# A Mamba-2 scan with a PReLU MLP: steps of the first group put in another order

## Chip, cores and metric

The kernel runs on one core of one Trainium2 chip. The metric is the device time of one execution, in microseconds (us); the time of a kernel is the median over several runs. The core has engines with a queue each: TensorE (PE, with its weight loads shown as PEld), VectorE (DVE), ScalarE (ACT), GpSimd (POOL), and SyncE (SP), which here only issues DMAs. Engines tell each other through semaphores that a step is done.

## What is computed

Two stages, the second on the output of the first. Cut to what matters:

```python
# x (4, 8, 768, 32), a (4, 8, 768), B and C (4, 8, 768, 16); chunks of 32 in the reference
for each chunk:
    cum = cumsum(log(clip(a, 1e-6, 1)))
    M = (C @ B^T) * exp(cum_i - cum_j) * (i >= j)       # per batch and head
    y = M @ x + (C @ state) * exp(cum)
    state = exp(sum(log a)) * state + sum_j B_j x_j exp(cum_end - cum_j)
# y, (batch, seq, heads * 32) = 3072 tokens x 256, goes into
h = y @ w_in                                            # 256 x 2048
g = max(h, 0) + alpha * min(h, 0)                       # PReLU with a slope for each column
out = g @ w_out                                         # 2048 x 256
```

## The kernel before

Everything is float32. The kernel works in chunks of 128 tokens. Two chunks are a **pair** (`pair(gp)`, gp = 0 to 11; six chunks, three pairs, to a batch), and two pairs, 512 tokens, are a **group** of the MLP (0 to 5). Pairs 0 and 1 feed group 0, pairs 2 and 3 feed group 1. Each engine runs its instructions in the order in which the code writes them (`manual_schedule`), so a line that is moved in the code is moved in the queues of all engines that it uses. The tile pools set only which buffer an allocation gets, and with it whose readers it waits for.

`pair(gp)` is a generator; `ssm(gp, n)` runs it up to its n-th next `yield`. For pairs 2 and 3 its steps are these:

1. *Transposes* of B and C on PE (L469), a copy of the result to `bc` on ACT (L472), the two masked copies `cz` on ACT (L484); then `pair_loads` makes `bn`, B times the decay to the chunk's end, on POOL (L385).
2. *Scans*: `decays(0)` and `decays(1)`, each four scans on DVE (L438), write the decay matrices `dec` of one chunk each, from `abc`, which a DMA has spread over the partitions.
3. *States*: `added` multiplies `xt` and `bn` on PE (L519), `states` brings the state forward on ACT (L544) and DVE (L547) and masks it on POOL (`sm`, L550), `c_decayed` makes `cd` on POOL (L487).
4. *Gram*: `products_bc`, eight matmuls of C and B into four tiles (L564); the fourth tile, for r = 3, is one of the two `hp` buffers.
5. *Products*: four multiplications of `dec` with the Gram tiles on DVE (L600), with a `yield` after the second; the order is r = 3, 2, 1, 0.
6. *y*: matmuls into two tiles (L616 for the state's part, L623 for `dec`), and copies to `xT`, the MLP's input, on ACT (L630).

The weights arrive in 16 **pieces** of 512 KB, in float64, and are turned into float32 on the chip. Pieces 0, 1 and 2 are `w_in` columns, and from there `w_out` and `w_in` take turns: the fourth piece is the first of `w_out`, the seventh is the fifth of `w_in`. A piece of `w_in` or `w_out` holds two of the 16 blocks f of d_ff. Its conversion has two parts. `convert_a` is the first: an absolute value (`wt`, L218) and a scaled copy of the lower bits (`wg`, L225 or L228) on ACT, and a clamp of `wt` on POOL (L220). `convert` is the rest: two steps on DVE (`wr`, L238 and L239) and an addition on POOL (L261), which writes the weights. `convert_next` takes the next piece, runs `convert` on it, then, unless `first=False`, `convert_a` on the piece two further on, and then lets SP load the piece six further on into the `raw` buffer that has come free (L202).

The first group is multiplied block by block. `hidden_two` does two blocks f for 256 tokens (L657): its matmuls, ACT's scaling by alpha (L663), and, in the function that it returns, the rest of the PReLU on DVE (L669). `hidden(0, f)` does one block for 512 tokens: two wide matmuls into an `hp` buffer, of which there are two (L642), ACT's scaling (L645) and DVE's maximum (L646). `output(f)` multiplies a block with `w_out` (L680). The loop over f from 4 to 15 writes, in this order: the loads of a pair and of `a`'s rows, a step of pair 2 for f up to 10, a step of pair 3 from f = 9 on, `hidden(0, f)`, `convert_next()`, `output(f - 4)`, and in four places a sum of weights on POOL (`weight_sums`, L709), whose tile is taken from the `raw` buffers.

`rows_clamp`, `rows_scan` and `rows_out` (L339 to L363) turn the second half of `a`'s rows into products: five instructions on DVE (L339, L346, L348, L358, L360) and two DMAs on SP (L363). Their results are read again by the loads of pair 6 and later. From group 1 on, `quad` and `product` do the MLP with seven products in place of eight (L766, L741).

Of the kernel before, what the change touches and what calls it, by code (L numbers as in the profile page):

```python
# [22 lines left out]
def kernel(  # L23
# [33 lines left out]
    Q = 128  # L57
# [35 lines left out]
    gp = ctx.enter_context(tc.tile_pool(name="gp", bufs=16))  # L93
# [6 lines left out]
    def bank(i):  # L100


        return ps_q.tile([P, 512], F32, name="bank", tag=f"q{i}")
# [5 lines left out]
    def ss_tile():  # L109
        if early[0] is None:  # L110
            return ps_s.tile([P, 512], F32, name="ss")
        early[0] += 1
        i = early[0] % (3 if ident_p else 4)
        return ps_s.tile([P, 512], F32, name="ss") if i < 2 else bank(i)
# [211 lines left out]
    held = {}  # L326
# [9 lines left out]
    def rows_clamp(i):  # L336
        rows = loads.pop(("r", i))
        d0 = prep.tile([RW, Q + 1], F32, name="r0")
        nc.vector.tensor_scalar(out=d0[:, :Q], in0=rows, scalar1=1e-6, scalar2=1.0,  # L339
                                op0=ALU.max, op1=ALU.min)  # L340
        held[i] = d0

    def rows_scan(i):

        d0 = held[i]
        nc.vector.memset(d0[:, Q:], 0.0)  # L346
        pr = prep.tile([RW, Q], F32, name="pr")
        nc.vector.tensor_tensor_scan(out=pr[:, ::-1], data0=d0[:, 1:][:, ::-1],  # L348
                                     data1=ends[:RW, ::-1], initial=0.0,
                                     op0=ALU.mult, op1=ALU.add)  # L350
        return pr
# [60 lines left out]
    def spare():  # L412

        return ps_h.tile([P, GT], F32, name="hp", tag="hp")

    def pair(gp):
# [7 lines left out]
        def decays(k):  # L424

            if abc:
                for w in range(2):
                    half_decays(k, w)
                return
            for w, t in enumerate(ahead.pop(k, None) or spread(z, k)):  # L430
                ws = slice(512 * w, 512 * w + 512)
                nc.vector.tensor_tensor_scan(out=dv[:, k, ws], data0=t, data1=ident_h[:, ws],
                                             initial=0.0, op0=ALU.mult, op1=ALU.add)

        def half_decays(k, w):
            for i in range(2):
                hs = slice((2 * w + i) * 2 * Q, (2 * w + i + 1) * 2 * Q)
                nc.vector.tensor_tensor_scan(out=dv[:, k, hs], data0=abc[k][:, hs],  # L438
                                             data1=ident_p[0], initial=0.0, op0=ALU.mult,
                                             op1=ALU.add)  # L440
# [36 lines left out]
        def spread_c():  # L477
            for e in range(2):
                o = cz[:, e].rearrange("p k t -> p (k t)")
                if gp == 0 and e == 1:  # L480
                    nc.gpsimd.tensor_scalar(out=o, in0=ct, scalar1=par[:, e : e + 1],
                                            scalar2=None, op0=ALU.mult)
                else:
                    nc.scalar.mul(o, ct, par[:, e : e + 1])  # L484

        def c_decayed():
            nc.gpsimd.tensor_tensor(out=cd.rearrange("p k t -> p (k t)"), in0=ct, in1=pf,  # L487
                                    op=ALU.mult)

        fine = gp >= 2 * GC // 2  # L490
        if not fine:
            spread_c()
        if gp == 0:
            rows_turn(0, held.pop("pr"))
            dps = spare()
# [3 lines left out]
        if gp == 1:  # L499
            c_decayed()  # L500
            dps = spare()
# [12 lines left out]
        def added(dps):  # L514
            dps = dps.rearrange("p (k m) -> p k m", m=P)
            for k in range(nk):
                for w in range(KC):
                    ws = slice(64 * w, 64 * w + 64)
                    nc.tensor.matmul(dps[ws, k], bn[:, k, ws], xt[:, k, w * P : (w + 1) * P],  # L519
                                     start=True, stop=True, tile_position=(0, 64 * w),  # L520
                                     skip_group_check=True)
            return dps

        if fine:
            for k in range(2):
                for w in range(2):
                    half_decays(k, w)
                    if k == 1 and w == 1:
                        spread_c()
                    yield  # L530
        else:
            decays(0)
            if gp == 1:
                dps = added(dps)
            if gp:
                yield
            if gp != 1:
                decays(1)

        def states(dps):  # L540
            for k in range(nk):
                old = state.get(b)
                if old is None:
                    nc.scalar.copy(out=new[:, k], in_=dps[:, k])  # L544
                else:
                    e = (k + 1) * Q - 1
                    nc.vector.scalar_tensor_tensor(out=new[:, k], in0=old, scalar=pf[:, e : e + 1],  # L547
                                                   in1=dps[:, k], op0=ALU.mult, op1=ALU.add)
                state[b] = new[:, k]
            nc.gpsimd.tensor_tensor(out=sm[:, :nk], in0=new[:, :nk],  # L550
                                    in1=hmask.unsqueeze(1).to_broadcast([P, nk, P]), op=ALU.mult)
            st.extend(sm[:, k] for k in range(nk))
            masked[b] = st[-1]

# [18 lines left out]
        def times(out, g):  # L575
            nc.gpsimd.tensor_tensor(out=out, in0=g, in1=out, op=ALU.mult)

        if gp == 0:
            gram = products_bc()
            dps = added(dps)  # L580
            yield
            c_decayed()
            times(dec[:, :, :2], one_less(gram))
        elif gp == 1:
            decays(1)
            gram = products_bc()
            g0 = one_less(gram)
            states(dps)
            times(dec[:, :, :2], g0)
        else:  # L590
            if not fine:
                yield
            states(added(ss_tile()))
            c_decayed()
            yield
            gram = products_bc()
        for i, r in enumerate(r for r in ((2, 3, 0, 1) if fine else (3, 2, 1, 0) if gp > 1 else range(4))
# [51 lines left out]
    def hidden_two(g, f, t0, hp):  # L649


        nt = GT // 2
        ts = slice(t0, t0 + nt)
        for i in range(2):
            fs = slice((f + i) * P, (f + i + 1) * P)
            for k in range(KC):
                nc.tensor.matmul(hp[:, i * nt : (i + 1) * nt], w_in[:, k, fs],  # L657
                                 xts[g][:, k, ts], start=(i == 0 and k == 0),
                                 stop=(k == KC - 1), skip_group_check=True)
        for i in range(2):  # L660
            if t0 == 0:
                gts[g, f + i] = gp.tile([P, GT], F32, name="gt")
            nc.scalar.mul(gts[g, f + i][:, ts], hp[:, i * nt : (i + 1) * nt],  # L663
                          s_alpha[:, f + i : f + i + 1])

        def rest():
            for i in range(2):
                gt = gts[g, f + i][:, ts]
                nc.vector.scalar_tensor_tensor(  # L669
                    out=gt, in0=hp[:, i * nt : (i + 1) * nt], scalar=s_mul[:, f + i : f + i + 1],  # L670
                    in1=gt, op0=ALU.mult, op1=ALU.max)
        return rest
# [233 lines left out]
    pieces = in_pieces[:2]  # L906
# [9 lines left out]
    def convert_next(first=True, **kw):  # L916


        i = done[0]
        if i < len(pieces):  # L920
            convert(*pieces[i], **kw)
            if first and i and i + 2 < len(pieces):
                convert_a(*pieces[i + 2])
            if loaded[0] == i + 6:
                load_next()
        done[0] += 1
# [13 lines left out]
    FIRST = 4  # L940
# [11 lines left out]
    prelus = [hidden_two(0, 0, 0, spare())]  # L952
# [6 lines left out]
    prelus[1]()  # L959
    ssm(1)  # L960
    convert_a(*pieces[3])
    prelus = [hidden_two(0, 0, 2 * Q, spare())]
    prelus[0]()
    prelus = [hidden_two(0, 2, 2 * Q, spare())]
    convert_a(*pieces[4])
    convert_next(first=False)
    prelus[0]()
    identity_bank()
    convert_a(*pieces[5])
    convert_next()  # L970
    in_steps = {8: 0, 10: 1, 12: 2, 14: 3}
    for f in range(FIRST, NF):
        if f in (5, 10):
            load_pair(3 + f // 10)
        if f == 5:
            load_rows(1)
        if f == 9:
            rows_clamp(1)
            held["pr"] = rows_scan(1)
            rows_out(1)  # L980
        if f <= 10:
            ssm(2)
        if f >= 9:
            ssm(3)
        hidden(0, f)
        convert_next()
        output(f - FIRST)
        if f in in_steps:
            weight_sums(wi, in_sums, 0, in_steps[f])
# [89 lines left out]
```

## Time and profile before

| what | value |
|---|---|
| median of 6 runs | 377.41 us |
| single runs | 376.75, 376.77, 377.04, 377.79, 378.97, 379.03 us |
| profiled execution | 376.77 us |
| its span, first to last instruction | 375.0 us |
| granted TensorE clock | 0.999 |
| bytes moved by DMA | 30.71 MB, mean 82 GB/s |

The span by stretches, in us, each of 15 us:

| stretch | PE busy | DVE busy | ACT busy | POOL busy | share of the DMA engines |
|---|---|---|---|---|---|
| 15 to 30 | 14.28 | 11.86 | 8.65 | 10.12 | 0.94 |
| 30 to 45 | 13.03 | 10.68 | 11.86 | 7.94 | 0.80 |
| 45 to 60 | 14.07 | 14.24 | 9.22 | 9.14 | 0.90 |
| 60 to 75 | 15.00 | 13.69 | 8.11 | 11.59 | 0.92 |
| 75 to 90 | 15.00 | 10.85 | 5.17 | 12.28 | 0.23 |

The loop over f runs from about 30 to 84 us. A line of a timeline gives the start and the length of one instruction, or of several of one kind that follow each other (xN), its engine, line and operation, the tile written and the tiles read, their shapes, and in brackets the idle time of the engine before it and what ended that. The listed length of an instruction runs into the next one, so the time that a step takes from the engine is the difference between two starts. A matmul's end is modelled.

### The profile page before, as it was taken

The page shows a single profiled execution, that of the slowest core. Times are in us where ns is not written, and L with a number is a line of the kernel's source. Part 1 is how long each engine was busy: PE and PEld are TensorE (multiplying, and loading weights), DVE is VectorE, ACT ScalarE, POOL GpSimd, SP SyncE. Part 2 cuts the span into 40 slices and gives each one's busy share as a digit, 9 for nine tenths or more (in the row PEclk, how much of TensorE's full clock was granted, in tenths as well). Part 3 has the DMA queues.
Part 4 walks back from the last instruction along what each step waited for, and adds up shares of the span by engine and source line. Part 5 has one row for each costly group of instructions (what it writes and reads, how often), then busy time and mean ns, then how long its engine had stood idle before and what let it go on. Part 6 is the DMA issues. An engine that isn't in the chain of part 4 may idle for free.

```text
span 375.0 us, 6178 instructions
## 1 busy us (share of the span) xinstructions
PE 365.4 (97%) x2223; PEld 294.5 (79%) x2223; DVE 242.6 (65%) x461; ACT 179.6 (48%) x384; POOL 203.2 (54%) x212
## 2 busy tenths in 40 slices
PE   8898999999999999999999999999999999999996
PEld 8675556668878788788788788788788888888884
DVE  7985899877547737747737847637847744544364
ACT  2658665526354444444445545435525525553541
POOL 4965475878857835625555435456354355264512
PEclk9999999999999999999999999999999999999999
DMA  7999697811008701002802702801801001001003
GB/s 157 226 211 354 132 307 160 170 46 58 28 26 172 140 3 56 2 0 45 167 3 48 162 2 39 173 0 30 154 29 27 3 0 20 12 0 30 1 0 84
DMA packets 121878, 30.71 MB, mean 82 GB/s; under 512 B 93736, under 2 KB 117752, under 8 KB 121848
## 3 DMA queue, kind: packets, MB, share of 16 engines
q1 hardware_dynamic: 116736, 29.74, 35.6%
q10 hardware_dynamic: 5112, 0.59, 1.1%
q8 instruction: 17, 0.28, 0.3%
q14 instruction: 13, 0.11, 0.1%
HBM read 26.98 MB, written 3.34 MB: 81 GB/s over the span
## 4 chain that ended last, share of the span: by engine, by line
PE 87%; DVE 5%; DMA 2%; POOL 2%; ACT 1%; issue 1%; POOLq 0%; DVEq 0%; ACTq 0%
PE hp L766 33%; PE bank L741 32%; PE bank L680 5%; PE hp L642 3%; PE ss L623 2%; DMA raw<-in_moe_w_in_dram 2%; PE ss L564 2%; PE ss L616 1%; DVE dec L438 1%; PE ss L519 1%; PE hp L564 1%; PE hp L657 1%; PE ss L469 1%; PE hp L270 1%; DVE wr L239 1%
## 5 line engine op out<-in xcount | busy, mean ns | idle before, releaser
L809 POOL TENSOR_TENSOR gt<-gt 128x512 f32<-128x512 f32 x58 | 73.6, 1270 | 31.7 <-DVE gt L751 24.8
L751 DVE SCALAR_TENSOR_TENSOR gt<-hp,s_mul,gt 128x256 f32<-128x256 f32 x120 | 52.6, 480 | 47.7 <-ACT gt L749 46.7
L741 PE MATMUL bank<-gt,w_out 128*128 128x256 f32 x320 | 82.5, 382 | 0.4 <-ACT o_sb L687 0.4
L749 ACT ACTIVATE gt<-hp,s_alpha 128x256 f32<-128x256 f32 x120 | 50.3, 470 | 47.2 <-PE hp L766 32.9
L741 PEld LDWEIGHTS bank<-gt,w_out 128*128 128x128 f32 x320 | 60.0, 190 | 11.2 <-issue 2.3
L800 POOL TENSOR_TENSOR gt<-gt 128x512 f32<-128x512 f32 x20 | 25.4, 1270 | 78.2 <-DVE gt L751 78.2
L741 PE MATMUL bank<-gt,ws 128*128 128x256 f32 x240 | 58.3, 379 | 0.0
L741 PEld LDWEIGHTS bank<-gt,ws 128*128 128x128 f32 x240 | 45.1, 190 | 5.8
L438 DVE TENSOR_TENSOR_SCAN dec<-abc,bank 128x256 f32<-128x256 f32 x80 | 48.1, 661 | 0.0
L766 PE MATMUL hp<-xs,w_in 128*128 128x256 f32 x160 | 42.8, 390 | 0.0
L766 PE MATMUL hp<-xT,w_in 128*128 128x256 f32 x160 | 41.9, 384 | 0.0
L766 PE MATMUL hp<-xs,ws 128*128 128x256 f32 x160 | 41.1, 379 | 0.0
L785 DVE TENSOR_TENSOR hp<-hp,u 128x512 f32<-128x512 f32 x20 | 14.0, 700 | 39.6 <-ACT u L783 39.6
L774 ACT COPY m<-hp 128x512 f32<-128x512 f32 x20 | 11.7, 586 | 51.5 <-PE hp L766 51.5
L766 PEld LDWEIGHTS hp<-xs,w_in 128*128 128x128 f32 x160 | 28.7, 189 | 7.7 <-issue 3.3
L766 PEld LDWEIGHTS hp<-xs,ws 128*128 128x128 f32 x160 | 30.4, 190 | 4.1
L766 PEld LDWEIGHTS hp<-xT,w_in 128*128 128x128 f32 x160 | 29.7, 190 | 5.0 <-issue 1.4
L680 PEld LDWEIGHTS bank<-w_out,gt 128*128 128x128 f32 x128 | 24.1, 190 | 11.4 <-issue 4.9
L680 PE MATMUL bank<-w_out,gt 128*128 128x256 f32 x128 | 30.7, 381 | 2.0 <-POOL w_out L261 2.0
L789 DVE TENSOR_TENSOR c<-hp,m 128x512 f32<-128x512 f32 x20 | 13.6, 682 | 19.2 <-PE hp L766 19.2
L642 PE MATMUL hp<-xT,w_in 128*128 128x512 f32 x48 | 23.2, 605 | 0.0
L783 ACT COPY u<-hp 128x512 f32<-128x512 f32 x20 | 11.7, 585 | 23.0 <-PE hp L766 23.0
(155 smaller groups left out, 555.1 us busy)
## 6 DMA issues: line engine op xcount, KB each, us to landing
abc<-z SPq DMA_DIRECT2D x20, 512.0 KB, 5.2
raw<-in_moe_w_in_dram SPq DMA_DIRECT2D x8, 512.0 KB, 4.8
raw<-in_moe_w_out_dram SPq DMA_DIRECT2D x8, 512.0 KB, 6.2
xt<-in_x_dram SPq DMA_DIRECT2D x24, 128.0 KB, 2.7
out_dram<-o_sb SPq DMA_DIRECT2D x32, 64.0 KB, 1.9
nat<-in_B_dram SPq DMA_DIRECT2D x22, 64.0 KB, 2.7
nat<-in_C_dram SPq DMA_DIRECT2D x22, 64.0 KB, 3.6
ap<-pf SPq DMA_DIRECT2D x11, 128.0 KB
```

Of the source, the lines that this page charges most:

```text
L438: nc.vector.tensor_tensor_scan(out=dv[:, k, hs], data0=abc[k][:, hs], data1=ident_p[0], initial=0.0, op0=ALU.mult, op1=ALU.add)
L642: nc.tensor.matmul(hp, w_in[:, k, f * P : (f + 1) * P], xts[g][:, k], start=(k == 0), stop=(k == KC - 1))
L680: nc.tensor.matmul(pos[0][t // 2][:, t % 2], gt[:, t * Q : (t + 1) * Q], w_out[:, f], start=(f == 0 and t % 2 == 0), stop=(f == NF - 1), s ...
L741: nc.tensor.matmul(ms[g][i][:, h], w, blocks[g, z][n][:, p], start=(q == 0 and h == 0), stop=(q == NQ - 1), skip_group_check=True)
L749: nc.scalar.mul(o[:, p], h[:, p], s_alpha[:, fs[p]])
L751: nc.vector.scalar_tensor_tensor(out=o[:, p], in0=h[:, p], scalar=s_mul[:, fs[p]], in1=o[:, p], op0=ALU.mult, op1=ALU.max)
L766: nc.tensor.matmul(to[:, p], w(2 * z + p), b, start=start and p == 0, stop=True, skip_group_check=True)
L774: nc.scalar.copy(out=m1, in_=A)
L785: nc.vector.tensor_tensor(out=Y, in0=Y, in1=u2, op=ALU.add)
L789: nc.vector.tensor_tensor(out=c22, in0=A, in1=m5, op=ALU.add)
L800: nc.gpsimd.tensor_tensor(out=tc_, in0=g22, in1=g12, op=ALU.subtract)
L809: eng.tensor_tensor(out=o, in0=x0, in1=x1, op=ALU.subtract)
```

## The change

In the first group's part of the program five things are put elsewhere.

- The fourth piece's `convert_next(first=False)` is written ahead of the third `hidden_two`, with which its DVE steps and its POOL addition come before the two PReLU parts of the second 256 tokens; before, they stood between the two.
- The fifth piece's `convert_next` no longer runs the seventh piece's `convert_a`; that is written behind `hidden(0, 4)`.
- In `pair`, the definition of `states` moves up, and for pairs 2 and 3 (gp > 1 and not `fine`) the states and `c_decayed` are run ahead of `decays(0)`. The `yield` that stood before them goes, so these pairs have one step less: pair 2 has its states at f = 5 (before: 7), its Gram matmuls and first products at 7 (8) and its y at 9 (10); pair 3 the same five steps later, states at 10 (12), Gram at 12 (13) and y at 14 (15).
- For the later pairs (`fine`) the order is what it was.
- The rows' three functions move from ahead of the steps of f = 9 to behind `convert_next()` of f = 11. On SP, their two DMAs then stand behind the loads of pair 4 instead of ahead of them.

No instruction is added or removed.

```diff
+        if fine:
+            ...
+        else:
+            if gp > 1:
+                states(added(ss_tile()))
+                c_decayed()
+            decays(0)
+            if gp == 1:
+                dps = added(dps)
+            if gp:
+                yield
+            if gp != 1:
+                decays(1)
...
         else:
-            if not fine:
-                yield
-            states(added(ss_tile()))
-            c_decayed()
+            if fine:
+                states(added(ss_tile()))
+                c_decayed()
             yield
             gram = products_bc()
...
     convert_a(*pieces[3])
-    prelus = [hidden_two(0, 0, 2 * Q, spare())]
-    prelus[0]()
-    prelus = [hidden_two(0, 2, 2 * Q, spare())]
+    convert_next(first=False)
+    hidden_two(0, 0, 2 * Q, spare())()
+    rest = hidden_two(0, 2, 2 * Q, spare())
     convert_a(*pieces[4])
-    convert_next(first=False)
-    prelus[0]()
+    rest()
     identity_bank()
     convert_a(*pieces[5])
-    convert_next()
+    convert_next(first=False)
     in_steps = {8: 0, 10: 1, 12: 2, 14: 3}
     for f in range(FIRST, NF):
         if f in (5, 10):
             load_pair(3 + f // 10)
         if f == 5:
             load_rows(1)
-        if f == 9:
-            rows_clamp(1)
-            held["pr"] = rows_scan(1)
-            rows_out(1)
         if f <= 10:
             ssm(2)
         if f >= 9:
             ssm(3)
         hidden(0, f)
+        if f == FIRST:
+            convert_a(*pieces[6])
         convert_next()
+        if f == 11:
+            rows_clamp(1)
+            held["pr"] = rows_scan(1)
+            rows_out(1)
         output(f - FIRST)
```

More of the change, by code (lines that the diff above doesn't have):

```diff
@@ L522, in added @@
             return dps
[L524 to L529, printed above, removed]
-                    yield
[L531 to L538, printed above, removed]
         def states(dps):
@@ L553, in states @@
             masked[b] = st[-1]
+        if fine:
+            for k in range(2):
+                for w in range(2):
+                    half_decays(k, w)
+                    if k == 1 and w == 1:
+                        spread_c()
+                    yield
[7 more added lines that the diff above has]
+            if gp:
+                yield
+            if gp != 1:
+                decays(1)
         def products_bc():
@@ L590, in pair @@
         else:
-            if not fine:
-                yield
-            states(added(ss_tile()))
-            c_decayed()
+            if fine:
+                states(added(ss_tile()))
+                c_decayed()
             yield
```

## The prediction

> **What bounds the kernel now.** I read the page's busy shares and its chain of waits first.
>
> ```profile
> PE 365.4 (97%) x2223; PEld 294.5 (79%) x2223; DVE 242.6 (65%) x461; ACT 179.6 (48%) x384; POOL 203.2 (54%) x212
> ...
> PE 87%; DVE 5%; DMA 2%; POOL 2%; ACT 1%; issue 1%; POOLq 0%; DVEq 0%; ACTq 0%
> ```
>
> TensorE is the bound: a microsecond counts only if it changes how long PE stands still. PE idles 375.0 - 365.4 = 9.6 us. Windows of 15 us put 5.7 of it before 60 us and 3.5 after 360 us; between, PE pauses once, 0.44 us at 110. So I read the timeline of PE from 26 to 90 us, where the change lies.
>
> ```profile
> 30.56 1.89 PE L642 MATMUL hp<-xT,w_in 128*128 128x512 f32 x4
> 33.89 1.99 PE L680 MATMUL bank<-w_out,gt 128*128 128x256 f32 x8 [1.44 <-POOL w_out L261]
> 41.58 1.99 PE L680 MATMUL bank<-w_out,gt 128*128 128x256 f32 x8 [0.53 <-POOL w_out L261]
> 48.69 0.48 PE L564 MATMUL ss<-cz,bc 32*128 32x256 f32 x1 [0.48 <-DVE state L547]
> 57.79 0.34 PE L616 MATMUL bank<-cd,sm 64*128 64x128 f32 x1 [0.45 <-DVE dec L600]
> 59.45 1.98 PE L642 MATMUL hp<-xT,w_in 128*128 128x512 f32 x4
> ```
>
> I write h4, o0 for the matmuls of hidden(0,4) and output(0), and so on. From start to next start, undisturbed after 60 us, h or o takes 1.72, or 1.82 next to another shape; L519 0.37 (four matmuls) or 0.59 (eight); a Gram block 1.08; four transposes 0.44; the y block 1.66 for pair 2 and 1.43 for pair 3. Against these, PE lost 1.51 before o0, 0.70 before o2, 0.10 at h7, 1.16 inside the Gram block and 0.51 before y: 4.0 us. That is all that this change can win; 59.45 to 84.34 us has no loss.
>
> Why those losses: ACT stood at the seventh piece's DMA, ahead of the bc copy and of h4's scaling; everything on DVE followed.
>
> ```profile
> 33.05 1.14 ACT L228 ACTIVATE wg<-raw,g_add,g_mul 128x256 f32<-128x256 uint16 x2
> 34.60 0.69 ACT L218 ACTIVATE wt<-raw 128x512 f32<-128x512 f32 x1 [0.41 <-DMA raw<-in_moe_w_in_dram]
> 35.75 0.57 ACT L472 COPY bc<-bank 128x512 f32<-128x512 f32 x1
> 37.17 0.67 ACT L645 ACTIVATE gt<-hp,s_alpha 128x512 f32<-128x512 f32 x1
> ```
>
> **The change, part by part.** Nothing is added or removed; every term is a wait.
>
> *Fourth piece ahead of PReLU.* Its L238/L239 now follow the PReLU at 26.06, so L239 starts when POOL's clamp ends (27.66 + 0.61), 28.30, and POOL's add runs 29.05 to 30.35 instead of from 32.51. o0 starts at 32.38 behind h4: -1.51. The PReLU at 29.47 starts as before (its ACT part ends 29.44).
>
> *Seventh piece behind h4.* bc follows L228 by 1.06 (as 53.31 to 54.37): 34.11; cz 0.60 later, h4's scaling 0.81 after that, 35.52; DVE's PReLU 0.70 later, 36.22 instead of 37.87. The seventh piece is wanted at 36.09 and had landed at 34.52.
>
> *States of pair 2 ahead of its scans.* L519 stands behind o0 on PE and needs bn.
>
> ```profile
> 34.94 1.27 POOL L261 TENSOR_TENSOR w_in<-wr,wg 128x512 uint32<-128x512 uint32 x1
> 36.30 0.61 POOL L220 TENSOR_SCALAR wt<-wt 128x512 f32<-128x512 f32 x1
> 36.99 0.64 POOL L385 TENSOR_TENSOR bn<-nat,prt 128x256 f32<-128x256 f32 x1
> ```
>
> POOL's order becomes: clamp of the sixth piece (ACT's L218 ends 33.16, so 33.22), add of the fifth 33.90, bn 35.25 to 35.89. PE is at L519 at 34.20 and waits to 35.93: +1.73. Queued behind it: h5 36.30, o1 38.12, h6 39.85, o2 41.56 (its weights are added by 39.5), Gram 43.38, h7 44.46. The Gram block's fourth tile now takes an hp buffer between h6 and h7, so h7 needs h6's PReLU read out. DVE: 36.22, L238 at +0.67, L239 at +0.52, state at +0.60, four scans at +0.26 (38.27), 2.33 for four scans, h5's PReLU 40.60, pair of L238/L239 1.78 with it, scans 42.38, h6's PReLU 44.71 to 45.43. Two L238 meet POOL (clamp, cd): +0.3. h7 starts 45.75: +1.29. Bounds: 45.4 without any meeting; 46.2 if the unexplained 0.46 before L239 at 39.48 repeats. What is erased: o2, the Gram split and y, since scans, states and products all end before PE comes.
>
> From h7: 1.82 + 1.73 + 1.71 + 1.82 + 1.66 + 0.44 = 9.18 brings h9 to 54.93. (In the profile h9 began 53.74 with y, 1.66, still to come.) Nothing else is late there: sm and cd, moved ahead on POOL, put the seventh piece's add at 42.5 to 43.8, and h8 wants it at 49.3; ACT, with the xT copies now ahead of bc and cz of pair 3, is done 56.6, and h9's scaling can start 56.95: cover 0.35, beyond which each delay would go straight into the next chain.
>
> *States of pair 3 ahead of its scans.* This decides. L519 now follows o5 on PE, two blocks after h9, and wants pair 3's bn; bn stands on POOL behind the first weight sum (ws), which takes a raw buffer and waits for the L238 behind h9's PReLU.
>
> ```profile
> 58.16 0.74 DVE L646 SCALAR_TENSOR_TENSOR gt<-hp,s_mul,gt 128x512 f32<-128x512 f32 x1
> 58.82 0.42 DVE L238 TENSOR_SCALAR wr<-raw 128x512 uint32<-128x512 uint32 x1
> 59.34 1.79 DVE L239 SCALAR_TENSOR_TENSOR wr<-wt,wr 128x512 uint32<-128x512 uint32 x1
> ...
> 59.32 1.27 POOL L709 TENSOR_TENSOR ws<-w_in 128x512 f32<-128x512 f32 x1 [2.67 <-DVE wr L238]
> 60.55 1.09 POOL L385 TENSOR_TENSOR bn<-nat,prt 128x256 f32<-128x256 f32 x1
> ...
> 66.53 0.66 PE L519 MATMUL ss<-xt,bn 128*64 128x128 f32 x8
> ```
>
> Today bn ends 61.64 and L519 comes at 66.53: 4.9 us of cover. After, the chain counts from h9's start: ACT 2.02 (59.45 to 61.47), DVE 0.72 (73.86 to 74.58), L238 0.67, ws 0.50, bn 1.23, bn itself 1.09, 0.05 to PE: 6.28. PE is there 1.82 + 1.82 = 3.64 after h9. Wait: +2.64, L519 at 61.21. Lower bound 2.19, with bn at its usual 0.64; upper 2.7.
>
> On that bn: L239 took 1.79 instead of 0.69 beside ws, and bn 1.09 beside L239. [...]
>
> *Later rows moved.* Five DVE instructions, 54.52 to 56.96, 2.44 us, leave the place before pair 2's products and now stand before pair 3's, behind the thirteenth piece's L239. h10 61.80, o6 63.62, h11 65.35, o7 67.06, Gram 68.88, h12 69.96, o8 71.78, h13 73.51; h13 wants the hp that the first product reads. DVE: state 62.2, scans 62.45, PReLU 64.78, two steps 65.43, scans 66.55, PReLU 68.88, two steps to 70.9 (L238 beside a weight sum, +0.3), rows to 73.34, product to 73.94. Wait +0.48 (bounds 0 and 0.8). y 77.5, h14 79.0, and the first matmul of the second group, 84.34 in the profile, at 86.4. On SP the rows' two DMAs now stand behind pair 4's loads and ahead of pair 5's, which start about 74 instead of 64.55. They took 8.7 us to issue; pair 5's bn runs at 103.68, so about 20 us cover it; without the cover it would cost what is late of the 9.5. Token sums on POOL: about 86.1, wanted by PE at 87.3; cover 0.5 after the first's 0.7.
>
> **Sum.** -1.51 - 0.70 - 0.10 - 1.16 - 0.51 + 1.73 + 1.29 + 2.64 + 0.48 = +2.2; by positions 86.4 - 84.34 = +2.1, which I take, as refills count there. Behind it PE is full, so the whole shift reaches the end. The profiled execution took 376.77 (span 375.0 and 1.77 around it): 378.9. It is 0.64 below the median of the runs, 377.41; a difference carries over, so 379.5.
>
> **The rivals.**
>
> *Not slower: the ws-bn wait does not bind.* If POOL had bn ready, the 2.64 falls: 2.1 - 2.64 = -0.5, 376.9 against the median. It decides from the point where bn is done before PE reaches L519, 3.64 after h9. For it: POOL is only 54% busy. Against: the 2.67 us idle before ws names DVE's L238, and the chain from h9 is longer than two PE blocks even with each link at its shortest. 0.08, half of it faster by over 0.5%, should PE's other two waits shrink too.
>
> *About the same: smaller losses, or fewer late runs.* Low ends without that: 2.1 - 0.35 - 0.45 - 0.48 = +0.8, 378.2. Or the runs before spread up to 379.03 because that seventh transfer lands at different times; after, it has 1.6 us of slack, so the median would be the sum's own 378.9. For: the chain of waits ran through that transfer (34.52); against: only one execution's trace is shown. 0.28.
>
> *Slower still.* DVE, with 0 to 0.5 us spare from 62 to 77 us, meets POOL more often, or the token sums come late: +1 more, 380.5. 0.09.
>
> **How the numbers follow.** The forecast, 379.5, has 0.55. Range 377.9 to 380.7: from the low ends to the third rival. A measurement of this kernel can tell about 0.5%, 1.9 us, from no change; faster by more 0.04, slower by more 0.62 (forecast, third rival, less a little at the border), same 0.34.
>
> **What would show it.** Right: o0 without a wait; L519 at about 36 waiting for bn by 1.7; h7 waiting for h6's PReLU by 1.3; L519 at about 61 waiting for bn by 2.6, the longest wait; no wait at Gram or y of pair 2. Wrong: L519 at 61 without a wait, or the second group starting before 85.2. Every step hangs on one fact, that engines take their instructions in the order written; where PE passed L519 while it waits, the forecast falls.

## The result and the profile after

| | before | after |
|---|---|---|
| median of 42 executions of before, 21 of after | 377.86 us | 380.57 us |
| profiled execution | 376.77 us | 381.57 us |
| its span | 375.0 us | 379.9 us |
| its granted TensorE clock | 0.999 | 0.996 |
| PE idle in the span | 9.6 us | 13.9 us |

The ratio of after to before is 1.0078, 95% interval 1.0061 to 1.0095: 2.9 us slower by the ratio and 2.7 by the medians, where +2.1 was forecast. Three executions far longer than the rest of their kernel (955.93 us of before, 472.96 of after, 804.47 of `warm_all_pauses`) count in no ratio. The first row of the profile page of after gives the busy time and share of each engine:

```profile
PE 366.0 (96%) x2223; PEld 294.3 (77%) x2223; DVE 241.6 (64%) x461; ACT 179.2 (47%) x384; POOL 202.3 (53%) x212
```

PE's idle time grew by 4.3 us, and its busy time by 0.6 with the same 2223 instructions. The second is no wait, and the prediction has no term of this kind. The timeline of PE in after, with the lines that it spoke of (h4, o0, L519, h7, L519 of pair 3, h10, o6, h13, and the first matmul of the second group):

```profile
30.94 1.89 PE L644 MATMUL hp<-xT,w_in 128*128 128x512 f32 x4
32.67 1.89 PE L682 MATMUL bank<-w_out,gt 128*128 128x256 f32 x8
36.35 0.44 PE L519 MATMUL ss<-xt,bn 128*64 128x128 f32 x4 [1.79 <-POOL bn L385]
...
46.69 1.99 PE L644 MATMUL hp<-xT,w_in 128*128 128x512 f32 x4 [1.74 <-DVE gt L648]
...
62.10 0.66 PE L519 MATMUL ss<-xt,bn 128*64 128x128 f32 x8 [2.56 <-POOL bn L385]
62.69 3.68 PE L644 MATMUL hp<-xT,w_in 128*128 128x512 f32 x4
66.20 1.89 PE L682 MATMUL bank<-w_out,gt 128*128 128x256 f32 x8
...
76.58 1.99 PE L644 MATMUL hp<-xT,w_in 128*128 128x512 f32 x4 [0.33 <-DVE dec L602]
...
89.08 1.03 PE L768 MATMUL hp<-xT,w_in 128*128 128x256 f32 x4
```

The waits before o0, o2, Gram and y of pair 2 are gone, and four new ones stand where the prediction put them. (This execution had h4 0.38 us later than the one before. In the traces of all kernels here h4 lies anywhere from 30.56 to 33.11 us, so distances from h4 are compared below.) New is the line at 62.69: h10, the same four matmuls as ever, takes 3.51 us from start to start instead of 1.82. The windows view of after says why (columns: the stretch, busy time of PE, PEld, DVE, ACT and POOL, granted clock, DMA share, GB/s):

```profile
62.00:63.00 1.00, 0.90 (x9) 0.73 (x10) 0.00 (x0) 0.20 (x1) 1.00 (x2) 0.86 1.08 119
63.00:64.00 1.00, 1.00 (x2) 0.48 (x2) 0.90 (x3) 0.07 (x1) 0.88 (x2) 0.50 1.08 234
64.00:65.00 1.00, 1.00 (x2) 0.37 (x2) 1.00 (x3) 0.00 (x0) 0.96 (x2) 0.50 1.01 232
65.00:66.00 1.00, 1.00 (x2) 0.34 (x1) 0.78 (x2) 0.00 (x0) 0.45 (x1) 0.50 0.48 141
66.00:67.00 1.00, 1.00 (x5) 0.72 (x4) 0.00 (x0) 0.60 (x2) 0.00 (x0) 0.93 0.02 8
```

The granted clock is 0.50 behind the longest wait; the trace's clock records give 62.73 to 66.14, 3.41 us. So the 2.56 us wait is paid for once as a wait and once more as matmuls at half speed. In the profile before, the clock is halved only at the very end, from 374.48.

The chain that sets the longest wait is the foreseen one. In the timelines of DVE and then of POOL in after:

```profile
59.24 0.42 DVE L238 TENSOR_SCALAR wr<-raw 128x512 uint32<-128x512 uint32 x1
59.76 1.79 DVE L239 SCALAR_TENSOR_TENSOR wr<-wt,wr 128x512 uint32<-128x512 uint32 x1
```

```profile
59.74 1.26 POOL L711 TENSOR_TENSOR ws<-w_in 128x512 f32<-128x512 f32 x1 [2.92 <-DVE wr L238]
60.96 1.09 POOL L385 TENSOR_TENSOR bn<-nat,prt 128x256 f32<-128x256 f32 x1
```

The weight sum starts as the L238 behind h9's PReLU ends, bn behind it, and PE's L519 starts 0.05 us after bn. Lengths (1.79, 1.09) are those of the profile before; what has changed is that PE now comes to L519 2.56 us before bn is done, where it came 4.9 us after.

The wait at h7 is longer than foreseen. DVE in after, behind h4:

```profile
36.58 0.75 DVE L648 SCALAR_TENSOR_TENSOR gt<-hp,s_mul,gt 128x512 f32<-128x512 f32 x1 [2.70 <-ACT gt L647]
37.25 0.84 DVE L238 TENSOR_SCALAR wr<-raw 128x512 uint32<-128x512 uint32 x1
38.62 0.69 DVE L239 SCALAR_TENSOR_TENSOR wr<-wt,wr 128x512 uint32<-128x512 uint32 x1 [0.53 <-DVE wr L238]
```

The gap of half a microsecond between the sixth piece's two steps is there again; elsewhere in the loop over f L239 follows 0.1 us behind L238. And this L238 takes 0.84 us, where it took 0.42 before: POOL's clamp of the seventh piece now starts just ahead of it. The two steps in the profile before, and the clamp in after:

```profile
38.54 0.42 DVE L238 TENSOR_SCALAR wr<-raw 128x512 uint32<-128x512 uint32 x1
39.48 0.69 DVE L239 SCALAR_TENSOR_TENSOR wr<-wt,wr 128x512 uint32<-128x512 uint32 x1 [0.52 <-DVE wr L238]
```

```profile
37.20 0.61 POOL L220 TENSOR_SCALAR wt<-wt 128x512 f32<-128x512 f32 x1 [0.90 <-ACT wt L218]
```

The work in front, on ACT, has moved as worked out (bc now stands directly behind L228, not behind a DMA):

```profile
33.45 1.12 ACT L228 ACTIVATE wg<-raw,g_add,g_mul 128x256 f32<-128x256 uint16 x2
34.47 0.57 ACT L472 COPY bc<-bank 128x512 f32<-128x512 f32 x1
35.07 0.91 ACT L484 ACTIVATE cz<-bc,par 128x256 f32<-128x256 f32 x2
35.88 0.67 ACT L647 ACTIVATE gt<-hp,s_alpha 128x512 f32<-128x512 f32 x1
```

### The profile page after: what moved, and what is told of

It is laid out like the page before. It is cut to its first block, busy times and chain, and to the rows that moved or that the text cites. A ratio compares the mean times of both kernels' runs of the same rounds, so it can differ in the third digit from the quotient of the medians.

```text
span 379.9 us, 6177 instructions
## 1 busy us (share of the span) xinstructions
PE 366.0 (96%) x2223; PEld 294.3 (77%) x2223; DVE 241.6 (64%) x461; ACT 179.2 (47%) x384; POOL 202.3 (53%) x212
## 4 chain that ended last, share of the span: by engine, by line
PE 82%; POOL 5%; DVE 4%; issue 4%; ACT 2%; DMA 1%; ACTq 1%; POOLq 0%; DVEq 0%
PE hp L768 33%; PE bank L743 31%; PE bank L682 3%; PE hp L644 2%; PE ss L625 2%; PE hp L659 2%; PE ss L567 2%; PE ss L618 1%; PE ss L519 1%; DMA nat<-in_B_dram 1%; POOL wt L220 1%; POOL w_out L261 1%; PE hp L567 1%; PE ss L469 1%; POOL w_in L261 1%
## 5 line engine op out<-in xcount | busy, mean ns | idle before, releaser
L644 PE MATMUL hp<-xT,w_in 128*128 128x512 f32 x48 | 24.9, 644 | 2.1 <-DVE gt L648 1.7
```

The lines of the kernel that those rows point to most:

```text
L644: nc.tensor.matmul(hp, w_in[:, k, f * P : (f + 1) * P], xts[g][:, k], start=(k == 0), stop=(k == KC - 1))
```

## The experiments

The time from h4 to the second group's first matmul leaves out the start of an execution. It is one execution's value, and in the three kernels that keep the seventh piece ahead of bc it still depends on when that piece's transfer lands: ACT waits for it 0.41 us in before, 1.20 in `rows_only` and 2.10 in `states_only`. All the kernels' profiled executions, with the periods of half clock between these two:

| kernel | ratio to before (95%) | h4 to second group, us | halved periods there |
|---|---|---|---|
| before | 1 | 53.78 | 0 |
| the prediction's positions for after | | 55.84 | |
| after | 1.0078 (1.0061 to 1.0095) | 58.14 | 1 |
| `after_again` | 1.0101 (1.0070 to 1.0133) | 57.64 | 1 |
| `pieces_only` | 0.9968 (0.9952 to 0.9985) | 52.53 | 0 |
| `states_only` | 1.0112 (1.0079 to 1.0144) | 58.75 | 1 |
| `rows_only` | 1.0007 (0.9990 to 1.0025) | 54.57 | 0 |
| `rows_back` | 1.0092 (1.0061 to 1.0123) | 59.17 | 2 |
| `bn_first` | 1.0033 (1.0017 to 1.0050) | 56.56 | 1 |
| `bn2_early` | 1.0137 (1.0110 to 1.0163) | 59.52 | 2 |
| `warm_in_pause` | 1.0128 (1.0101 to 1.0156) | 58.40 | 0 |
| `warm_half` | 1.0070 (1.0046 to 1.0095) | 56.29 | 0 |
| `warm_all_pauses` | 1.0071 (1.0049 to 1.0093) | | |
| `states_late_rows_end` | 0.9947 (0.9928 to 0.9966) | 51.68 | 0 |
| `sixth_steps_early` | 0.9912 (0.9887 to 0.9938) | 50.07 | 0 |

### One part of the change alone

`pieces_only`: before, with the two pieces' moves (the diff's last hunk without the rows).

```diff
+    convert_next(first=False)
+    hidden_two(0, 0, 2 * Q, spare())()
...
+    convert_next(first=False)
...
+        if f == FIRST:
+            convert_a(*pieces[6])
```

> Of the change only the two pieces are moved (fourth ahead of PReLU, seventh's first part behind h4); states and rows stay as before. Theory (the pieces win, the states lose): no wait at o0, ACT's scaling of h4 at about 35.9, the second group starts 1.7 to 2.0 us earlier than in the kernel before: 375.9 to 376.2, ratio 0.994 to 0.996. Rival (the pieces' gain is given back at the Gram block and at y, where DVE is the bound anyway): less than 0.7 us, ratio 0.998 to 1.001.

Measured: 0.9968, faster, between the theory's range and the rival's; from h4 to the second group it takes 1.25 us less. PE's waits from 18 to 115 us, by the waits view (total, times, longest):

```profile
PE bank L680 <- POOL w_out L261: 1.0, 1, 1.0
PE ss L564 <- DVE state L547: 0.5, 1, 0.5
PE bank L616 <- DVE dec L600: 0.4, 1, 0.4
```

The 1.5 before o0 is gone; the waits at o2, Gram and y, which hang on DVE, remain or grow (o2's from 0.53 to 1.00), so a part of the gain is given back there.

`states_only`: before, with the states of pairs 2 and 3 ahead of their scans, and a `yield` less.

```diff
+            if gp > 1:
+                states(added(ss_tile()))
+                c_decayed()
             decays(0)
...
-            if not fine:
-                yield
-            states(added(ss_tile()))
-            c_decayed()
+            if fine:
+                states(added(ss_tile()))
+                c_decayed()
```

> Of the change only the states of pairs 2 and 3 are moved ahead of their scans; pieces and rows stay as before. Theory: waits at pair 2's L519 (about 1.9 us), at h7 (1 to 1.7 us) and at pair 3's L519 (2.2 to 2.6 us), with half clock behind the last; time 381.0 to 382.0, ratio 1.008 to 1.011. Rival (the states move loses nothing by itself, it is the seventh piece behind h4 or the rows that loses): ratio 0.998 to 1.003.

Measured: 1.0112. All of the loss is here. PE's timeline (o0, L519 of pair 2, h5):

```profile
34.37 1.99 PE L682 MATMUL bank<-w_out,gt 128*128 128x256 f32 x8 [1.43 <-POOL w_out L261]
...
38.92 0.44 PE L519 MATMUL ss<-xt,bn 128*64 128x128 f32 x4 [2.56 <-POOL bn L385]
39.29 3.33 PE L644 MATMUL hp<-xT,w_in 128*128 128x512 f32 x4
```

Here the first L519 waits 2.56 us, and it is h5 behind it that runs at half clock (0.50 by the windows view, from about 39.8 to 43.2). Pair 3's L519 waits 2.56 too, at 65.10, and no halving follows. The first wait is longer than after's 1.79 because the parts touch each other: with the seventh piece in its old place, pair 2's bn stands on POOL behind that piece's clamp, and the clamp behind ACT, which waits for the transfer:

```profile
36.80 0.66 ACT L218 ACTIVATE wt<-raw 128x512 f32<-128x512 f32 x1 [2.10 <-DMA raw<-in_moe_w_in_dram]
```

`rows_only`: before, with the rows moved.

```diff
-        if f == 9:
-            rows_clamp(1)
-            ...
         convert_next()
+        if f == 11:
+            rows_clamp(1)
+            ...
```

> Of the change only the rows are moved, from f = 9 to f = 11; pieces and states stay as before. Theory (DVE is full from 56 to 73 us, so 2.44 us taken out ahead of pair 2's products are put in ahead of pair 3's): PE's wait of 0.45 us at y of pair 2 goes, and nothing else is won or lost: ratio 0.998 to 1.000. Rival (the rows cost pair 3 the 2.44 us that they no longer cost pair 2): PE waits for pair 3's products, ratio 1.002 to 1.006.

Measured: 1.0007, no difference; y's wait goes (the rows stood ahead of its products), and no gain shows. The interval would hide 0.4 us, and the trace cannot tell, as the seventh piece's transfer landed later in it than in before's.

`rows_back`: after, with the same hunk undone, the rows at f = 9 again.

> Kernel: the changed kernel with the later rows back at their old step, that is the moves of the pieces and of the states without that of the rows. Theory (the rows ahead of the fourth pair's product are worth h13's 0.33 us wait at most, and VectorE does the rows' work either way): ratio 1.0070 to 1.0080, as 0.9968 of the pieces times 1.0112 of the states gives 1.0080. Rival (the rows in the stretch of the third pair's Gram are what costs): 1.004 to 1.006. Rival (with the rows back the second pair's y waits for L238 again, 0.4 us): 1.009.

Measured: 1.0092 beside 1.0101 for `after_again` on the same chip, not to be told apart. h13's wait goes, as the first theory said, but the interval holds its 1.0070 to 1.0080 and 1.009 alike. The profiled execution shows two halvings: h7 behind its own 1.73 us wait (3.36 us from start to start instead of 1.82), and the second behind L519's 2.56 us (L519 itself 0.87 instead of 0.59, h10 3.18 instead of 1.82):

```profile
46.47 3.57 PE L644 MATMUL hp<-xT,w_in 128*128 128x512 f32 x4 [1.73 <-DVE gt L648]
...
63.57 0.95 PE L519 MATMUL ss<-xt,bn 128*64 128x128 f32 x8 [2.56 <-POOL bn L385]
```

The parts multiply to 0.9968 x 1.0112 x 1.0007 = 1.0087, within after's interval.

### Taking a wait away

`bn_first`: after, with the first weight sum one step later, so that pair 3's bn does not stand behind it.

```diff
-    in_steps = {8: 0, 10: 1, 12: 2, 14: 3}
+    in_steps = {9: 0, 10: 1, 12: 2, 14: 3}
```

> The first weight sum goes from f = 8 to f = 9, so that POOL makes pair 3's bn ahead of it; all else as in the changed kernel. Theory (the wait at pair 3's L519 is the one that decides, and the half clock behind it comes from it): the wait of 2.56 us at about 62 us and the 3.4 us at clock 0.50 both go; the first matmul of the second group starts 3.9 to 4.3 us earlier than in the changed kernel's trace, and the time falls by about as much, to 376.3 to 376.9, ratio to the kernel before 0.995 to 0.998. Rival (DVE bounds this stretch, so the wait only moves to the Gram block or to h13 of pair 3): less than 1.5 us is won, ratio above 1.003.

Measured: 1.0033, in the rival's range; some 1.7 us come back (1.0078 - 1.0033 = 0.0045 of 377.86). L519 of pair 3 no longer waits: the ws-bn chain was its cause. But PE's timeline (L519, h7, h13) shows where part of the gain went:

```profile
36.69 0.44 PE L519 MATMUL ss<-xt,bn 128*64 128x128 f32 x4 [1.79 <-POOL bn L385]
47.02 3.64 PE L644 MATMUL hp<-xT,w_in 128*128 128x512 f32 x4 [1.74 <-DVE gt L648]
75.34 1.98 PE L644 MATMUL hp<-xT,w_in 128*128 128x512 f32 x4 [1.24 <-DVE dec L602]
```

h13 waits 1.24 instead of 0.33. From h9's PReLU on, DVE has next to no idle time (states, eight scans, three PReLU, pieces, rows), and its timeline ends with the rows right ahead of the product that h13 wants:

```profile
72.42 1.46 DVE L348 TENSOR_TENSOR_SCAN pr<-r,ends 96x128 f32<-96x128 f32 x1
73.80 0.77 DVE L358 TENSOR_TENSOR_SCAN rpf<-r,zeros 96x128 f32<-96x128 f32 x1
74.60 0.69 DVE L602 TENSOR_TENSOR dec<-hp,dec 128x512 f32<-128x512 f32 x1
```

So 2.56 us of PE wait were worth about 1.7: behind them stands DVE's chain, which lets no more through.

`bn2_early`: after, with pair 2's bn made before the loop.

```diff
     identity_bank()
+    bns[2] = pair_loads(2)
     convert_a(*pieces[5])
```

> In the changed kernel POOL makes pair 2's bn ahead of the clamps and the fifth piece's addition. Theory (h7 waits for DVE's chain and not for PE): the wait of 1.8 us at pair 2's L519 goes, PE comes to h7 as much earlier and waits there 3.5 us instead of 1.74, h9 starts where it did; the time stays as in the changed kernel, or is up to 1.5 us more where the longer pause halves the clock: ratio 1.006 to 1.012. Rival (each wait counts for itself): 1.8 us less, ratio 1.002 to 1.004.

Measured: 1.0137, above the theory's range and far above the rival's: slower than after (1.0078; but `after_again`'s interval reaches 1.0133), although its first wait (1.79) is gone. PE's timeline (h7, pair 3's L519):

```profile
48.33 3.51 PE L644 MATMUL hp<-xT,w_in 128*128 128x512 f32 x4 [2.91 <-DVE gt L648]
...
65.26 1.12 PE L519 MATMUL ss<-xt,bn 128*64 128x128 f32 x8 [2.56 <-POOL bn L385]
```

h7 waits 2.91 instead of 1.74: h7 hangs on DVE's chain from h4's PReLU, not on PE's position, so most of what PE wins ahead of it is lost there again (and 0.44 at o2). And both waits are followed by a halved clock (h7 takes 3.35 us from start to start, L519 1.05 and h10 2.89, instead of 1.82, 0.59 and 1.82).

### Filling a wait with dummy matmuls

`warm_in_pause`: the same wait, without the pause: dummy matmuls ahead of pair 3's L519, into the tile that it writes first.

```diff
         def added(dps):
+            if gp == 3:
+                keep_warm(dps, 10)
```

> Ten matmuls of ones, 0.215 us each (2.15 us), are put ahead of pair 3's L519 in the changed kernel; they write the tile that L519 then overwrites, so the output is the reference's. Theory (standing still makes the clock halve): L519 still starts when bn is there, about 62 us, the clock stays at 1.00, and the time falls by 1.4 to 1.7 us although work is added: ratio 1.003 to 1.004. Rival (the half clock has another cause): clock 0.50 is there again, and the time is that of the changed kernel or up to 0.3 us more, ratio 1.007 to 1.009.

Measured: 1.0128, outside both ranges. The fill was twice too long; in the timeline of PE, 20 matmul records of 0.22 us where 10 were written:

```profile
60.18 4.48 PE L270 MATMUL ss<-warm 128*128 128x256 f32 x20
64.59 0.66 PE L521 MATMUL ss<-xt,bn 128*64 128x128 f32 x8
```

L521 (L519 in after) comes 1.7 us after its bn (61.76 + 1.09). The clock stays at full speed here (1.0 in the mean), but the run says nothing on its price; `warm_half` has 5 in place of 10.

> As the run with ten matmuls of ones, which took 4.4 us where 2.15 were meant (a matmul of 256 columns leaves two records of 0.22 us each): five here, 2.2 us, so that they fit into the pause of 2.56 us. Theory: pair 3's L519 starts when bn is there, at h9 + 6.2; the clock does not halve behind it. If the half clock costs what it lasts for (1.7 us), ratio 1.003 to 1.005; if DVE's chain behind it (scans, rows, products) hides most of that, as equal times with and without a halved clock in the run with bn first suggest, ratio 1.006 to 1.008.

Measured: 1.0070, not to be told from after's 1.0078. Its profiled execution has the clock at full speed (1.0 in the mean) throughout the loop; h7, L521 and h13 in PE's timeline:

```profile
46.67 1.98 PE L646 MATMUL hp<-xT,w_in 128*128 128x512 f32 x4 [1.32 <-DVE gt L650]
...
62.07 0.66 PE L521 MATMUL ss<-xt,bn 128*64 128x128 f32 x8 [0.40 <-POOL bn L385]
...
75.11 1.98 PE L646 MATMUL hp<-xT,w_in 128*128 128x512 f32 x4 [0.57 <-DVE dec L604]
```

From L521 to h13 it takes 13.04 us, in after 14.48: the halving costs 1.44 us there, in this pair of executions. In `after_again` the same stretch takes 13.99, so there it costs 0.95. What carries it on is h10's PReLU, the next step of DVE's chain; in DVE's timeline of after, DVE waits 1.34 us for it:

```profile
67.12 0.75 DVE L648 SCALAR_TENSOR_TENSOR gt<-hp,s_mul,gt 128x512 f32<-128x512 f32 x1 [1.34 <-ACT gt L647]
```

In `warm_half` DVE does not wait there; in `after_again` it waits 0.83 us, as the halving began later and slowed h10 by 1.13 us instead of 1.69. h4 to the second group takes 56.29, against the prediction's 55.84. (h7's wait is 1.32 in this execution and not 1.74: 0.42 less, as much as L238 is longer beside POOL's clamp in after.) The ratio lies in the range for a cost mostly hidden, but does not decide: three of the six executions have a mean clock of 0.995, by which they were halved at some other place.

`warm_all_pauses` fills three: 4 dummies ahead of pair 2's L519, 3 ahead of its Gram, 5 ahead of pair 3's L519.

```diff
         def added(dps):
+            if gp in (2, 3):
+                keep_warm(dps, 4 if gp == 2 else 5)
...
         def products_bc():
             ...
+            if gp == 2:
+                keep_warm(gram[0].rearrange("p k h t -> p (k h t)"), 3)
```

> Kernel: the changed kernel with dummy matmuls in TensorE's pauses: 4 (1.76 us) ahead of the second pair's L519, 3 (1.32 us) ahead of its Gram, 5 (2.2 us) ahead of the third pair's L519. Theory (the waits alone cost what the positions give, and halvings add up to 1.5 us in the executions that have them): no halving before the tail, clock 0.998 or more in all runs, ratio about 1.0065, spread of the runs small. Rival (a halving is hidden behind VectorE's chain and costs nothing): the same ratio as the changed kernel, 1.0078. Rival on the other side (dummies outlast the pauses): 1.009 or more, with L519 starting later than the bn that releases it.

Measured: 1.0071; the clock is 0.997 to 1.0 in all executions compared, and they lie within 0.6 us (380.29 to 380.88). No trace of it is read. The ratio lies between the theory's 1.0065 and the rival's 1.0078 and does not decide. `after_again`, on the same chip, has 0.991 to 0.996 and spreads over 3.4 us (380.22 to 383.66, median 381.22).

> The changed kernel once more, beside the others on the same chip. All theories: ratio 1.0061 to 1.0095; its runs with a granted clock of 0.998 or more are shorter than those at 0.995 by 0.5 to 1.5 us if halvings cost time, and equal to them if these are hidden.

Over the 27 executions of after in the study, by the mean clock (one halved period takes 0.5 x 3.41 / 380 = 0.0045 from it):

| mean clock | halved periods by it | executions | median us | from, to |
|---|---|---|---|---|
| 0.999 | 0 | 1 | 379.76 | |
| 0.993 to 0.996 | 1 | 22 | 380.58 | 379.86, 381.96 |
| 0.985 to 0.991 | 2 or 3 | 4 | 383.21 | 382.79, 383.66 |

So after is hardly ever without a halving. What one costs depends on what stands behind it: in `bn_first`, four executions at clock 1.0 (378.15 to 378.31) and seven at 0.993 to 0.994 (378.15 to 378.83) are nearly equal, and one, at 0.995, took 380.33. That one is the profiled execution, with its halving at h7, and there it costs its full length: DVE stands idle for 3.81 us ahead of h9's PReLU, so its chain starts behind the delay and cannot take it up. Where the seven were halved is not recorded. In `states_only` the two at 1.0 took 379.98 and 380.49, the four at 0.996 took 381.72 to 383.39. A second period can lie outside the loop: `after_again`'s profiled execution has 0.991, two periods, and between 28 and 100 us only one stretch of slowed matmuls, behind pair 3's L519.

### Keeping what wins

`states_late_rows_end`: the pieces moved as in the change (the diff is against after), the states only ahead of the second chunk's scans, with the old number of steps, and the rows at f = 15.

```diff
-            if gp > 1:
-                states(added(ss_tile()))
-                c_decayed()
             decays(0)
...
+            if gp > 1:
+                states(added(ss_tile()))
+                c_decayed()
             if gp != 1:
                 decays(1)
...
+            if not fine:
+                yield
...
-        if f == 11:
+        if f == NF - 1:
```

> The two pieces as in the change; the states of pairs 2 and 3 ahead of their second scan with all later steps where they were before (Gram at f = 8 and 13); the rows at f = 15, where DVE stood still for 2.58 us. Theory: bn is ready before each L519, the Gram block of pair 2 no longer waits 1.2 us for the state, y no longer waits 0.45 us for the products; with the 1.2 us of the pieces the second group starts about 2.7 us earlier than before: ratio 0.991 to 0.994. Rival (DVE is the bound from 36 to 60 us and gives it back elsewhere): no better than the pieces alone, 0.996 to 0.998.

Measured: 0.9947, faster than before, between the theory's range and the rival's; waits of 0.43 at o2 and 0.76 at h8 remain, both of DVE's chain behind h4.

`sixth_steps_early`: the same, with the sixth piece's DVE steps issued in DVE's idle time ahead of h4's PReLU.

```diff
+    convert_b(*pieces[5])
     in_steps = {8: 0, 10: 1, 12: 2, 14: 3}
```

> Kernel: the order of states_late_rows_end (pieces moved as in the change, states of the third and fourth pair only ahead of their second scans, later rows at the end of the group), and the sixth piece's two VectorE steps issued right behind the fifth's transfer step, so that they run in VectorE's 2.7 us of idle time before the PReLU of h4 and not behind it. Theory (VectorE's chain behind h4 sets when o2 and h8 can start): the steps' 1.2 us and the 0.46 us gap ahead of L239 leave that chain, the waits of o2 (0.43) and h8 (0.76) in states_late_rows_end go, ratio to before 0.990 to 0.993. Rival (the two waits have other releasers, w_out and the product, that come no earlier): no better than 0.9947. Rival on the other side: the earlier steps meet GpSimd or delay h4's PReLU, h4's output matmul waits 0.5 to 1.2 us more, ratio 0.996 to 0.999.

Measured: 0.9912 (374.20 us), by the ratio 3.3 us faster than before, and in the theory's range. DVE's timeline:

```profile
33.91 0.83 DVE L238 TENSOR_SCALAR wr<-raw 128x512 uint32<-128x512 uint32 x1
34.85 1.57 DVE L239 SCALAR_TENSOR_TENSOR wr<-wt,wr 128x512 uint32<-128x512 uint32 x1
36.72 0.75 DVE L651 SCALAR_TENSOR_TENSOR gt<-hp,s_mul,gt 128x512 f32<-128x512 f32 x1 [0.30 <-ACT gt L650]
```

The two steps end before ACT has h4's scaling ready, and the gap of 0.5 us ahead of L239 is not there at this place. o2 no longer waits and h8 waits 0.45. From h4 to the second group it takes 50.07: 3.71 us less than in the profile before, where PE lost 4.0. This version beats both kernels.

## Why the prediction had the waits right and their sum too small

Two steps of the sum failed: h7's wait, put at 1.29 us, measured 1.74; and the clock behind a pause, put at nothing without a reason, cost 1.69 us at h10 in the profiled execution, of which 1.44 reached h13.

- **What bounds: right.** PE's waits made the result; no other engine's share had to be known.
- **The losses erased: right.** o0, o2, the Gram split and y of pair 2 are without a wait in after. `pieces_only` shows that the pieces alone do this for o0 only.
- **Pair 2's L519: right.** +1.73 foreseen, 1.79 measured, with bn as releaser.
- **h7: mis-sized.** +1.29 foreseen, 1.74 measured, with the releaser foreseen (h6's PReLU). The working took the gap ahead of the sixth piece's L239 (0.46 there; 0.52 by the row) as an accident of one execution and put it at the range's upper end (46.2). It is 0.51 to 0.53 in the five traces whose DVE timeline shows the two steps at this place: no accident, so the upper end was the value to take. By it DVE's chain is 0.43 us longer; another 0.12 is POOL's clamp, which lengthened one L238 by 0.42, where 0.3 was put down for two such meetings. PE comes 0.1 later too, so h7's wait is 0.45 longer, and that stays in all positions behind.
- **Pair 3's L519: right.** +2.64 foreseen, 2.56 measured; bn took 1.09 in after and in `states_only`, beside an L239 of 1.79, as in the row. `bn_first` shows the cause. The rival in which this wait does not bind falls.
- **Rows and h13: right within its bounds.** +0.48 foreseen (0 to 0.8), 0.33 measured. `rows_back` and `rows_only` show that the move is worth nothing that can be measured.
- **Missing: the clock behind a pause.** The sum counted each wait for its length alone. In the profiled execution the clock behind pair 3's L519 costs h10 3.51 - 1.82 = 1.69 us, of which 1.44 reach h13. So h4 to the second group is 58.14 - 55.84 = 2.30 us longer than foreseen; h7, h10 and the small differences of the other waits give 0.06 + 0.45 - 0.08 + 1.69 - 0.15 = 1.97 of it, and the rest is spread over the blocks. With that one pause filled and no halving (`warm_half`, with the shorter wait at h7) it is 56.29.
- **The time.** For the profiled execution the sum gave 378.9, and 381.57 was measured: 0.38 of the 2.7 between lies ahead of h4, 2.30 behind it. For the median 379.5 was forecast and 380.57 measured. 0.45 of the 1.07 between is the median of before, 377.41 over six executions and 377.86 over 42; 0.45 is h7's term; some 0.2 remain for the clock and all else. That is less than the traces' 1.44 or 0.95, and the ratios of after and `warm_all_pauses` (1.0078, 1.0071) do not tell the clock's share of the median from nothing. How large it is in the mean stays open.
- **"A difference carries over": not shown.** This step added 0.64, as before's profiled execution was faster than the median (over 42 executions by 1.1). The second rival put before's spread down to the seventh piece's transfer, for which the changed kernel would not wait, and named 378.9. The traces speak for it in part: in the old order ACT waits for that transfer 0.41, 1.20 and 2.10 us, in the new order 0 (after, `after_again`) and 0.26 (`warm_half`). As far as that holds, the difference does not carry over, and the clock's share is larger by as much. No run parts the two.

The third rival, +1 us from DVE and POOL meeting, named a time close to the measured one by luck: the meetings that the trace shows on its path (L238 0.84 and 0.80 instead of 0.42) exceed what the forecast had for them by 0.2 us in all, and the token sums made nothing wait.

## What to carry to other kernels

Before a consumer is moved ahead in an in-order queue, follow its operand's producer back to the event that starts it, and compare that time with the consumer's new place: here both new L519 waits were readable so, 0.06 and 0.08 us off. Where a change has several parts, cost and try them one by one: a gain of 0.3% was hidden under a loss of 1.1%. And a wait on TensorE is not priced by its length alone: look at the granted clock behind it (here 0.50 for 3.41 us behind a wait of 2.56), and at what hangs on the matmuls that it slows.

## What the runs showed of the hardware

**A halving lasted 3.41 us, and the length of a pause alone does not decide on it.** By the clock records of after's trace the granted clock is 0.50 from 62.73 to 66.14; by the windows views it is so in `states_only` from about 39.8 to 43.2 and in `bn_first` from about 47.2 to 50.6. Two starts in one trace lay a multiple of that apart: in after 62.73 and, at the end of the execution, 380.17 (93.0 times 3.413); in `rows_back` the slowed steps put them about 17.1 us apart (5.0 times). PE's pauses compare so, with the `hidden` step behind each, from its start to the next one's:

| execution, pause | idle, us | step behind it, us (1.82 undisturbed) |
|---|---|---|
| after, L519 of pair 3 | 2.56 | h10 3.51 |
| `states_only`, L519 of pair 2 | 2.56 | h5 3.12 |
| `after_again`, L519 of pair 3 | 2.56 | h10 2.95 |
| `bn_first`, h7 | 1.74 | h7 3.43 |
| `rows_back`, h7 | 1.73 | h7 3.36 |
| `states_only`, L519 of pair 3 | 2.56 | h10 1.82 |
| after, h7 | 1.74 | h7 1.83 |
| `bn_first`, L519 of pair 2 | 1.79 | h5 1.82 |
| `rows_back`, L519 of pair 2 | 1.80 | h5 1.82 |
| `warm_half`, L521 of pair 2 | 1.81 | h5 1.82 |

Pauses of 1.73, 1.74 and 2.56 us had a halving behind them, and pauses of 1.74, 1.79 to 1.81 and 2.56 had none. So a pause of one length cost that length alone at one place and more at another, and what decides is not shown. Beside h7's pause stand Gram's matmuls of 32 rows, beside L519's full ones; whether that matters was not tried.

**A gap of half a microsecond on DVE belongs to a place.** Between L238 and L239 behind h4's PReLU there are 0.51 to 0.53 us in each of the five traces whose DVE timeline shows that place (before 0.52, after 0.53, `pieces_only` 0.52, `states_only` 0.51, `states_late_rows_end` 0.52), and 0.1 where the same two steps stand ahead of that PReLU (`sixth_steps_early`, from 34.74 to 34.85). POOL's clamp of the next piece is not it: in `states_only` it had ended at 38.15, and the gap began at 41.11. The cause stays open.
